# Local scores of tiles 6 and 11 moved one step behind the values, and the last output block stored in halves

## The chip, the cores and the metric

The kernel runs on one core of a Trainium2 chip. The metric is the device time of one execution in microseconds. It is measured several times per kernel, and one more execution is profiled. Engines are named as in the profile: PE (TensorE; PEld are its weight loads), DVE (VectorE), ACT (ScalarE), POOL (GpSimd) and SP (SyncE, which issues the DMAs).

## The reference

Attention with two kinds of heads, followed by a feed-forward layer on all tokens:

```python
batch, n_heads, seq, head_dim = (8, 8, 576, 64)
scores = scale * np.matmul(q, k.transpose(0, 1, 3, 2))
rel = pos[:, None] - pos[None, :]
mask_local = (rel >= 0) & (rel < stride)
mask_strided = (rel >= 0) & (pos[None, :] % stride == pos[:, None] % stride)
masks = np.stack([mask_local if h < H // 2 else mask_strided for h in range(H)], axis=0)
attn = softmax(np.where(masks, scores, -1e9))
x = (attn @ v) as 4608 tokens x 512 channels
h = x @ w_in
out = (0.5 * h * (1 + erf(h / sqrt(2)))) @ w_out
```

The stride is 32, w_in is 512 x 2048 and w_out 2048 x 512, all in float32.

## The kernel before

The 4608 tokens are cut into 12 tiles of 384. A tile has three local jobs of 128 tokens each (heads 0 to 3), strided rows (heads 4 to 7) and 16 steps of feed-forward, one for each 128 of the 2048 hidden channels. Steps are numbered through: n = 16 t + f. Values are kept as a high part rounded for PE and a low remainder (xh and xl, gh and gl), so each product is three matmuls.

- **Feed-forward step n.** `ffn_h` (L619 to L621) makes 12 matmuls of 128x384 into a PSUM bank H. `ffn_g` applies Gelu on ACT (L628), rounds to gh on ACT (L630) and subtracts to gl on DVE (L632). `ffn_o` of step n-2 (L658 to L660) makes 9 matmuls of 128x512 into three banks O. `store` copies O to SBUF on ACT (L665) and sends it from SP (L667) once a tile is full.
- **Strided heads.** They run on DVE alone: dot products row by row (L494, two instructions each), and accumulations of weighted values (L536), cut into small pieces that `run_strided` hands out step by step; a transpose (L544), then xh on ACT (L236) and xl on DVE (L238).
- **Local heads.** A `band_job` has seven parts. Part 0 is the score matmuls (L297; the page counts 96 passes for the three jobs of a tile). Parts 1 to 3 are the masked minimum on DVE (L311), the exponential on ACT (L315), and on DVE the quotients and a transpose, with 8 small DMAs per job from SP that set up the tile `band` (L326). Part 4 is the value matmuls (L337; 48 passes per tile). Parts 5 and 6 copy the result to xh on ACT (L236) and subtract xl on DVE (L238).

A tile's scores stand in two PSUM banks S0 and S1 of 512 columns: 128 columns for each of the three jobs. The last 128 columns of the *next* tile's two banks take the values of the third job of *this* tile; the other two jobs' values go to a bank X. Before, `score_banks` took a tile's two banks in the step in which its scores were made.

The order on ACT and PE is the order of the code in `step(n)`: first `visit(n)` (value matmuls of one tile, then score matmuls of the next), then `ffn_h(n)` and its Gelu, then the softmax parts due in this step, strided pieces, and `ffn_o(n-2)`. Which step visits which tile is set by three tables:

```python
    FIRST, VISIT = 2, 13
    value_at = {ready[t - 1] + VISIT: t for t in range(2, NTILE)}
    score_at = {ready[1] + FIRST: 2, **{n: t + 1 for n, t in value_at.items()}}
    soft_at = {}
    for n, t in score_at.items():
        for i in range(JPT if t < NTILE else 0):
            for p in (1, 2, 3):
                soft_at.setdefault(n + p + i * (2 if t == 2 else 4), []).append((t * JPT + i, p))
```

With `ready[t] = 16 t`, step 77 has the values of tile 5 and the scores of tile 6, step 157 the values of tile 10 and the scores of tile 11, and step 173 the values of tile 11 alone. DVE's, SP's and POOL's order is worked out by the framework's scheduler from the same code; the framework also sets the semaphore waits between engines, for any two accesses of one PSUM tile.

Of the kernel before, what the change touches and what calls it, by code (L numbers as in the profile page):

```python
# [24 lines left out]
P = 128  # L25
STRIDE = 32
TT = 384
# [55 lines left out]
def attn_ffn_kernel(ctx: ExitStack, tc: tile.TileContext, qk, vl, qka, va, qs, ks, vs, w, out):  # L83
    nc = tc.nc
# [4 lines left out]
    NT, DM = out.shape  # L89
# [4 lines left out]
    NTILE = NT // TT  # L94
# [32 lines left out]
    def slot(name, shape, dtype=F32):  # L127

        return wpool.tile(shape, dtype, name=name, tag="w")
# [149 lines left out]
    def score_banks(t):  # L279
        return [ps_a.tile([P, DM], F32, name=f"S{j}_{t}", tag=f"S{j}") for j in range(2)]  # L280
# [165 lines left out]
    for vi in range(NA, NV):  # L446
        n = VISITS[vi][2]
# [162 lines left out]
    hps, gs, ops_ = {}, {}, {}  # L610
    ready = [t * NF for t in range(NTILE)]
# [23 lines left out]
    def runs(t, a):  # L635

        res = []
        for c in range(0, P, 32):
            _, b, r = ROWS[TR * t + (a * P + c) // 32]
            r = b * S + 32 * r  # L640
            if res and res[-1][2] + res[-1][1] - res[-1][0] == r:
                res[-1][1] = c + 32
            else:
                res.append([c, c + 32, r])
        return res
# [16 lines left out]
    def store(t):  # L662
        for a in range(TT // P):
            ob = opool.tile([P, DM], F32, name=f"ob_{t}_{a}", tag="ob", bufs=3)
            nc.scalar.copy(ob, ops_[t][a])  # L665
            for c0, c1, r0 in runs(t, a):
                nc.sync.dma_start(out[r0:r0 + c1 - c0, :], ob[c0:c1, :])  # L667


    strided = []  # L670
# [2 lines left out]
    for u in range(U0, NU + 1):  # L673
        for v, what, names in ((u, strided_qk, "qk"), (u - 1, strided_av, "v")):
            if U0 <= v < NU:
                vi, _, r0, nr, t, _ = PLACE[v]
# [39 lines left out]
    t = slot("pbig", [P, 4 * DM])  # L716
# [27 lines left out]
    for i in range(JPT):  # L744
        t = opool.tile([P, DM], F32, name=f"first_{i}", tag="ob", bufs=3)
# [3 lines left out]
    def ffn(n):  # L749
        ffn_h(n)  # L750
        yield
        yield from ffn_g(n)
        yield
        ffn_o(n)
        if n % NF == NF - 1:
            yield
            store(n // NF)
# [39 lines left out]

    FIRST, VISIT = 2, 13  # L800
    value_at = {ready[t - 1] + VISIT: t for t in range(2, NTILE)}
    score_at = {ready[1] + FIRST: 2, **{n: t + 1 for n, t in value_at.items()}}
    soft_at = {}
    for n, t in score_at.items():
        for i in range(JPT if t < NTILE else 0):
# [5 lines left out]
    banks = {}  # L811
# [6 lines left out]
    def part(x, *which):  # L818

        for p in which:  # L820
            if p == 0:
                local[x] = [band_job(x, bts[x % NBT], banks), 0]
            assert local[x][1] == p
            local[x][1] += 1
            next(local[x][0], None)
            if p == 0:
                load_jq(x + 3)

    def visit(n):

        t = value_at.get(n, 0)
        if score_at.get(n, 0):
            banks[score_at[n]] = score_banks(score_at[n])
        for i in range(JPT if t else 0):
            part(t * JPT + i, 4)
        for i in range(JPT if score_at.get(n, NTILE) < NTILE else 0):
            part(score_at[n] * JPT + i, 0)
# [12 lines left out]
    def step(n):  # L850


        c = n // NF
        visit(n)
        if NB <= n < NS:
            ffn_h(n)
            for _ in ffn_g(n):
                pass
        old = len(splits)
        while old and n >= xfree[splits[0][0]]:  # L860
            for _ in splits.pop(0)[1]():
                pass
            old -= 1
        softmaxes(n)
        flush_exps(NU)
        if c + 1 < NTILE:
            a, e = ready[c] + (1 if c == 0 else 0), ready[c + 1]
            part_of = min(1.0, max(0.0, (n - a + 1) / (e - a - 3)))
            need = last[c] + (last[c + 1] - last[c] + sum(taken[a:e - 3])) * part_of - sum(taken[a:min(n + 1, e - 3)])
            share = (n + 1 - NB) / (ready[-1] - 2 - NB)  # L870
            run_strided(max(need, (tot + sum(taken)) * share - sum(taken[:n + 1])))
        if n == NS + 1:
            ffn_o(n - 3, n - 2)
        elif n >= NB + 2 and n < NS:
            ffn_o(n - 2)
        if n >= NB + 2 and (n - 2) % NF == NF - 1:
            store((n - 2) // NF)
# [71 lines left out]
```

## Time and profile before

| what | value |
|---|---|
| runs | 875.07, 878.97, 878.74 us; median 878.74 |
| profiled execution | 877.5 us, its span 875.7 us |
| mean granted TensorE clock | 0.990 |
| busy: PE, DVE, ACT | 856.4 us (98%), 706.2 us (81%), 482.7 us (55%) |
| chain that ended last | PE 90%, DVE 3%, DMA 3%, ACT 2% |
| H matmuls L619, L620, L621 | 768 each, 261.6, 259.4 and 260.6 us |
| O matmuls L658, L659, L660 | 576 each, 224.4, 227.7 and 228.3 us |
| score matmuls L297 | 1056, 13.8 us |

How to read it: the span goes from the first to the last instruction on any engine; the execution's own time has a little more around it. The chain is followed back from the last instruction to what released it at each step. "Issue" is time in which an engine waited for nothing that the profile shows. Busy shares are averages over the whole span; what a place is worth is read from the timeline there.

### The profile page before, as it was taken

How to read it: one execution, taken by the hardware profiler on the slowest of the kernel's cores; microseconds unless marked ns; L12 is line 12 of the kernel's file. 1: busy time of each engine (PE TensorE's matmuls, PEld its weight loads, DVE VectorE, ACT ScalarE, POOL GpSimd, SP SyncE). 2: the span in 40 equal slices, each digit the busy share in tenths (PEclk: the TensorE clock that was granted, in tenths of full speed). 3: DMA queues.
4: the chain of work that ended last, by engine and by line, in shares of the span. 5: the costliest groups of instructions: out<-in, count | busy, mean ns of one | idle time of the engine just before them, and what ended most of it. 6: DMA issues, size and time to landing. Idle time of an engine off the chain costs nothing.

```text
span 875.7 us, 19634 instructions
## 1 busy us (share of the span) xinstructions
PE 856.4 (98%) x6082; PEld 771.0 (88%) x6082; DVE 706.2 (81%) x4901; ACT 482.7 (55%) x1001; POOL 17.5 (2%) x89
## 2 busy tenths in 40 slices
PE   5999999999999999999999999999999989999998
PEld 4888898999999999999999899989989979989997
DVE  6998999998989997889999979899799993751111
ACT  7888585566465375357355445556547435443222
POOL 5000100000000000000000000000000000000000
PEclk9799999999999999999999999999999999999999
DMA  9695301320310320310311121131032002000001
GB/s 352 223 380 200 115 24 37 108 76 8 128 47 9 101 97 10 104 44 8 97 50 58 55 76 47 34 122 48 9 101 80 12 30 59 18 6 12 26 1 37
DMA packets 34552, 66.67 MB, mean 76 GB/s; under 512 B 6800, under 2 KB 16528, under 8 KB 34448
## 3 DMA queue, kind: packets, MB, share of 16 engines
q1 hardware_dynamic: 34448, 65.43, 22.1%
q8 instruction: 48, 0.79, 0.4%
q14 instruction: 56, 0.46, 0.2%
HBM read 51.64 MB, written 9.44 MB: 70 GB/s over the span
## 4 chain that ended last, share of the span: by engine, by line
PE 90%; DVE 3%; DMA 3%; ACT 2%; SPq 1%; issue 1%; DVEq 0%; ACTq 0%
PE H L619 15%; PE O L659 14%; PE O L660 14%; PE H L621 14%; PE H L620 14%; PE O L658 14%; PE X_L L337 1%; PE S L297 1%; DMA ws<-in_w_dram 1%; DMA qka<-in_qka_dram 1%; DMA sk<-in_ks_dram 1%; DVE ws L161 1%; SPq L326 1%; PE S L337 1%; DVE w L169 1%
## 5 line engine op out<-in xcount | busy, mean ns | idle before, releaser
L628 ACT ACTIVATE H<-H 128x384 f32<-128x384 f32 x192 | 91.3, 476 | 363.0 <-PE H L621 304.3
L619 PE MATMUL H<-xh,w 128*128 128x384 f32 x768 | 261.6, 341 | 1.5 <-DVE gl L632 1.4
L621 PE MATMUL H<-xh,w 128*128 128x384 f32 x768 | 260.6, 339 | 0.0
L620 PE MATMUL H<-xl,w 128*128 128x384 f32 x768 | 259.4, 338 | 0.4 <-DVE xl L238 0.4
L536 DVE SCALAR_TENSOR_TENSOR acc<-sv,sc,acc 128x64 f32<-128x64 f32 x1158 | 249.5, 275 | 0.7
L660 PE MATMUL O<-w,gl 128*128 128x512 f32 x576 | 228.3, 396 | 0.0
L659 PE MATMUL O<-w,gh 128*128 128x512 f32 x576 | 227.7, 395 | 0.0
L658 PE MATMUL O<-w,gh 128*128 128x512 f32 x576 | 224.4, 390 | 0.0
L494 DVE CUSTOM_DVE_ANT_0 junk<-sq,sk 128x64 f32<-128x64 f32 x1290 | 203.8, 217 | 3.5 <-DMA sk<-in_ks_dram 2.4
L632 DVE TENSOR_TENSOR gl<-H,gh 128x384 fp32r<-128x384 f32 x192 | 105.7, 551 | 106.0 <-ACT gh L630 105.1
L619 PEld LDWEIGHTS H<-xh,w 128*128 128x128 f32 x768 | 145.4, 189 | 11.1 <-DVE gl L632 1.7
L620 PEld LDWEIGHTS H<-xl,w 128*128 128x128 f32 x768 | 145.3, 189 | 8.5 <-DVE xl L238 0.8
L621 PEld LDWEIGHTS H<-xh,w 128*128 128x128 f32 x768 | 145.0, 189 | 0.1
L660 PEld LDWEIGHTS O<-w,gl 128*128 128x128 f32 x576 | 108.1, 188 | 23.7 <-DVE gl L632 0.6
L659 PEld LDWEIGHTS O<-w,gh 128*128 128x128 f32 x576 | 108.1, 188 | 18.2
L658 PEld LDWEIGHTS O<-w,gh 128*128 128x128 f32 x576 | 108.5, 188 | 17.3
L494 DVE DVE_READ_ACCUMULATOR2_ANT sc<- 128x1 f32 x1290 | 103.6, 80 | 0.0
L630 ACT CAST gh<-H 128x384 fp32r<-128x384 f32 x192 | 92.2, 480 | 6.1
L628 ACT ACT_TABLE_LOAD x60 | 77.0, 1283 | 1.0
L504 ACT ACT_TABLE_LOAD x35 | 44.9, 1283 | 0.6
L315 ACT ACTIVATE PT_L<-P_L,nm_L 128x64 f32<-128x64 f32 x132 | 44.2, 337 | 0.3
L315 ACT ACT_TABLE_LOAD x24 | 30.8, 1283 | 0.5
(114 smaller groups left out, 488.7 us busy)
## 6 DMA issues: line engine op xcount, KB each, us to landing
ws<-in_w_dram SPq DMA_DIRECT2D x16, 1023.8 KB, 10.1
qk<-in_qk_dram SPq DMA_DIRECT2D x36, 320.0 KB, 5.0
out_dram<-ob SPq DMA_DIRECT2D x34, 256.0 KB, 2.4
vl<-in_vl_dram SPq DMA_DIRECT2D x36, 192.0 KB, 4.3
sk<-in_ks_dram SPq DMA_DIRECT2D x8, 576.0 KB, 5.5
sv<-in_vs_dram SPq DMA_DIRECT2D x8, 576.0 KB, 3.9
band<-PT_L SPq DMA_DIRECT2D x240, 16.0 KB, 1.8
sq<-in_qs_dram SPq DMA_DIRECT2D x4, 576.0 KB, 4.4
```

The source lines that it names most:

```text
L315: nc.scalar.activation(pv[:, :, h, :], p1[:, h * 2 * QB:(h + 1) * 2 * QB].rearrange("p (c t) -> p c t", c=2), AF.Exp, bias=nm[:, h:h + 1], ...
L494: nc.vector.tensor_tensor_reduce(junk, sq[vi, "q"][:, r0 + r, :], sq[vi, "k"][:, c, :], 1.0, 0.0, ALU.mult, ALU.add, ss[u][:, r, c:c + 1])
L536: nc.vector.scalar_tensor_tensor(acc[:, r, :], sq[vi, "v"][:, c, :], wgt, acc[:, r, :], ALU.mult, ALU.add)
L619: nc.tensor.matmul(hp, w1[f][:, 0, c, :], xh[:, c, :], start=(c == 0), stop=False)
L620: nc.tensor.matmul(hp, w1[f][:, 0, c, :], xl[:, c, :], start=False, stop=False)
L621: nc.tensor.matmul(hp, w1[f][:, 1, c, :], xh[:, c, :], start=False, stop=(c == NC - 1))
L628: nc.scalar.activation(hp, hp, AF.Gelu)
L630: nc.scalar.copy(gh, hp)
L632: nc.vector.tensor_tensor(gl, hp, gh.bitcast(F32), ALU.subtract)
L658: nc.tensor.matmul(o, gh[:, sl], w2[f][:, 0, :], start=(f == 0), stop=False)
L659: nc.tensor.matmul(o, gh[:, sl], w2[f][:, 1, :], start=False, stop=False)
L660: nc.tensor.matmul(o, gl[:, sl], w2[f][:, 0, :], start=False, stop=(f == NF - 1))
```

## The change

`LATE` names the tiles 6 and 11. Their scores (part 0) are made in the step behind the one that has the values of the tile before: step 78 instead of 77, and step 158 instead of 157. Softmax parts follow, since `soft_at` counts from `score_at`. The two S banks are still taken in the values' step, since the values' third job writes into them. In `store`, the last 128 tokens of the last tile are copied in two halves of 256 columns, the first on ACT and the second on DVE, each with its own DMA.

```diff
-            nc.scalar.copy(ob, ops_[t][a])
-            for c0, c1, r0 in runs(t, a):
-                nc.sync.dma_start(out[r0:r0 + c1 - c0, :], ob[c0:c1, :])
+            halves = 2 if t == NTILE - 1 and a == TT // P - 1 else 1
+            for i in range(halves):
+                cs = slice(i * DM // halves, (i + 1) * DM // halves)
+                if i:
+                    nc.vector.tensor_copy(ob[:, cs], ops_[t][a][:, cs])
+                else:
+                    nc.scalar.copy(ob[:, cs], ops_[t][a][:, cs])
+                for c0, c1, r0 in runs(t, a):
+                    nc.sync.dma_start(out[r0:r0 + c1 - c0, cs], ob[c0:c1, cs])
...
-    FIRST, VISIT = 2, 13
+    FIRST, VISIT, LATE = 2, 13, (6, 11)
     value_at = {ready[t - 1] + VISIT: t for t in range(2, NTILE)}
-    score_at = {ready[1] + FIRST: 2, **{n: t + 1 for n, t in value_at.items()}}
+    score_at = {ready[1] + FIRST: 2, **{n + (t + 1 in LATE): t + 1 for n, t in value_at.items()}}
...
         t = value_at.get(n, 0)
-        if score_at.get(n, 0):
-            banks[score_at[n]] = score_banks(score_at[n])
+        new = t + 1 if t else score_at.get(n, 0)
+        if new and new not in banks:
+            banks[new] = score_banks(new)
```

PE, tile 6: the last value matmuls and the first score matmuls, with the semaphores that each waits for. S_6 are tile 6's two banks, O_2 is the last of the three output banks. Before:

```order
L337 MATMUL S_6_5581<-band,vl_4551 64x64
L337 MATMUL S_6_5582<-band,vl_4551 64x64 [waits PE_49]
L337 MATMUL S_6_5582<-band,vl_4551 64x64 x3
L297 MATMUL S_6_5581<-qk_4569 32x64
L297 MATMUL S_6_5582<-qk_4569 32x64
```

Now, behind the value matmuls, 12 matmuls of H and 9 of O:

```order
L658 MATMUL O_2_4975<-w_1222,gh_5504 128x512
L659 MATMUL O_2_4975<-w_1222,gh_5504 128x512
L660 MATMUL O_2_4975<-w_1222,gl_5505 128x512
L297 MATMUL S_6_5581<-qk_4569 32x64 [waits DVE_49]
L297 MATMUL S_6_5582<-qk_4569 32x64 [waits DVE_49]
```

The scores stood directly behind the values and now stand a step later, and the first one into each bank waits for DVE: the counts waited for are those of the two `xl<-S_6` below. At tile 11 the same two rows stand in the same way.

DVE, tile 6: gl of step 77, then xl of the three jobs' values (X_L: two jobs, S_6: the third job in two halves). Before (between the gl of the step before and this one stand 22 of L536, L544 and 23 pairs of L494):

```order
L632 TENSOR_TENSOR gl_5682<-H_5668,gh_5681 128x384
L494 ISA junk_3_5_6127,sc_6038<-sq_5459,sk_5461 128x64
...
L238 TENSOR_TENSOR xl_4817<-X_L_5583,xh_4816 128x2x128 x2
L238 TENSOR_TENSOR xl_4817<-S_6_5581,xh_4816 128x128
L311 ISA P_L_5728,nm_L_5730<-S_6_5581,bmaskNone 128x64
...
L238 TENSOR_TENSOR xl_4817<-S_6_5582,xh_4816 128x128
```

Now (between the two gl stand 22 of L536, L544 and 6 pairs of L494):

```order
L632 TENSOR_TENSOR gl_5628<-H_5614,gh_5627 128x384
L494 ISA junk_2_1_6050,sc_5994<-sq_5459,sk_5461 128x64
...
L238 TENSOR_TENSOR xl_4817<-X_L_5583,xh_4816 128x2x128 x2
L238 TENSOR_TENSOR xl_4817<-S_6_5581,xh_4816 128x128
L238 TENSOR_TENSOR xl_4817<-S_6_5582,xh_4816 128x128
```

Each fence shows the first of four L494 pairs that stand between gl and xl. Up to the gl of step 76 DVE's order is the same in both kernels; then gl and xl stand 17 pairs earlier, and the two xl of S_6 follow each other.

DVE, tile 11: the same place at step 157. Before:

```order
L503 TENSOR_TENSOR sc_11469<-sc_11469,m_11610 128x36
L536 SCALAR_TENSOR_TENSOR acc_11328<-sv_10030,sc_10676,acc_11328 128x64 x25
L632 TENSOR_TENSOR gl_10974<-H_10960,gh_10973 128x384
L536 SCALAR_TENSOR_TENSOR acc_11328<-sv_10030,sc_10676,acc_11328 128x64 x2
L238 TENSOR_TENSOR xl_10070<-X_L_10881,xh_10069 128x2x128 x2
L238 TENSOR_TENSOR xl_10070<-S_11_10879,xh_10069 128x128
```

Now:

```order
L503 TENSOR_TENSOR sc_11469<-sc_11469,m_11570 128x36
L536 SCALAR_TENSOR_TENSOR acc_11319<-sv_10030,sc_10676,acc_11319 128x64 x5
L632 TENSOR_TENSOR gl_10926<-H_10912,gh_10925 128x384
L536 SCALAR_TENSOR_TENSOR acc_11319<-sv_10030,sc_10676,acc_11319 128x64 x2
L238 TENSOR_TENSOR xl_10070<-X_L_10881,xh_10069 128x2x128 x2
L238 TENSOR_TENSOR xl_10070<-S_11_10879,xh_10069 128x128
L238 TENSOR_TENSOR xl_10070<-S_11_10880,xh_10069 128x128
```

Of the 25 accumulations ahead of gl, 20 stand behind it now, and up to L503 the order is the same.

On ACT there are 126 table loads where there were 120, since softmax parts and strided exponentials fall into other steps. At the end, DVE's copy of the second half waits for ACT's count after the first half, and SP issues the two DMAs one behind the other.

## Rows read from the trace of the kernel before

**Rows 1.** The page, part 1: busy us (share) xinstructions of each engine

```profile
PE 856.4 (98%) x6082; PEld 771.0 (88%) x6082; DVE 706.2 (81%) x4901; ACT 482.7 (55%) x1001; POOL 17.5 (2%) x89
```

**Rows 2.** Timeline of PE, 707 to 724 us: start us, us, engine, line, operation

```profile
707.53 0.33 PE L619 MATMUL H<-xh,w 128*128 128x384 f32 x1
...
717.44 0.30 PE L297 MATMUL S<-qk 64*32 64x64 f32 x4 [2.94 <-issue]
...
723.52 0.33 PE L619 MATMUL H<-xh,w 128*128 128x384 f32 x1
```

**Rows 3.** Stretches: length, busy of PE, PEld, DVE, ACT, POOL; PEclk, DMA, GB/s

```profile
718.60:722.05 3.45, 3.45 (x12) 3.25 (x11) 3.06 (x16) 0.84 (x2) 0.00 (x0) 0.51 0.02 5
82.50:87.30 4.80, 3.42 (x18) 3.20 (x19) 4.77 (x20) 4.61 (x9) 0.00 (x0) 1.00 0.09 21
```

**Rows 4.** Timeline of PE, tile 6's visit: first H matmul of steps 76, 77, 78

```profile
358.36 0.33 PE L619 MATMUL H<-xh,w 128*128 128x384 f32 x1
...
365.29 0.44 PE L619 MATMUL H<-xh,w 128*128 128x384 f32 x1
...
369.58 0.33 PE L619 MATMUL H<-xh,w 128*128 128x384 f32 x1
```

**Rows 5.** Timeline of PE, values-only visit: first H matmul of steps 171 to 174

```profile
777.95 0.33 PE L619 MATMUL H<-xh,w 128*128 128x384 f32 x1
...
782.14 0.33 PE L619 MATMUL H<-xh,w 128*128 128x384 f32 x1
...
787.97 0.44 PE L619 MATMUL H<-xh,w 128*128 128x384 f32 x1
...
792.26 0.33 PE L619 MATMUL H<-xh,w 128*128 128x384 f32 x1
```

**Rows 6.** The chain of waits at a visit: start us, us, engine and line

```profile
432.55 1.08 PE X_L L337 x32
433.63 0.47 PE S L337 x16
```

**Rows 7.** DMA queues, whole span and then 714.8 to 716 us: packets, MB, share

```profile
q8 instruction: 48, 0.79, 0.4%
...
q8 instruction: 1, 0.02, 5.4%
```

**Rows 8.** Timeline of DVE, 368 to 373 us (tile 6)

```profile
368.48 0.22 DVE L494 CUSTOM_DVE_ANT_0 junk<-sq,sk 128x64 f32<-128x64 f32 x1
...
370.96 0.55 DVE L632 TENSOR_TENSOR gl<-H,gh 128x384 fp32r<-128x384 f32 x1
...
372.01 0.75 DVE L238 TENSOR_TENSOR xl<-X_L,xh 128x256 fp32r<-128x256 f32 x2
372.68 0.28 DVE L238 TENSOR_TENSOR xl<-S,xh 128x128 fp32r<-128x128 f32 x1
```

**Rows 9.** Timeline of DVE, 716 to 724 us (tile 11)

```profile
716.68 4.98 DVE L536 SCALAR_TENSOR_TENSOR acc<-sv,sc,acc 128x64 f32<-128x64 f32 x25
722.19 0.56 DVE L632 TENSOR_TENSOR gl<-H,gh 128x384 fp32r<-128x384 f32 x1 [0.54 <-ACT gh L630]
...
723.06 0.75 DVE L238 TENSOR_TENSOR xl<-X_L,xh 128x256 fp32r<-128x256 f32 x2
```

**Rows 10.** Timeline of ACT, 365 to 370 us (tile 6)

```profile
369.11 0.47 ACT L236 CAST xh<-S 128x128 fp32r<-128x128 f32 x2
```

**Rows 11.** Timeline of DVE, 790 to 794 us (values-only visit)

```profile
792.81 0.48 DVE L238 TENSOR_TENSOR xl<-S,xh 128x128 fp32r<-128x128 f32 x2
```

**Rows 12.** ACT's table loads (count, busy us, mean ns); last copy on ACT; output DMAs

```profile
L628 ACT ACT_TABLE_LOAD x60 | 77.0, 1283 | 1.0
...
871.90 0.59 ACT L665 COPY ob<-O 128x512 f32<-128x512 f32 x1 [0.77 <-PE O L660]
...
DMA to landing us min/median/max: 2.0/2.4/3.3
```

## The prediction

> **What bounds the kernel now.** I read the page's engine table first: PE is busy 98% of the span [rows 1], so only what makes PE idle, slows it or adds work to it moves the end. Next I read PE's timeline at the edited places. PE's stream is a row of equal steps of 4.19 us (from one step's first H matmul to the next, 777.95 to 782.14 [rows 5]). In one step of each tile stands a "visit": 48 value passes of this tile (L337), then 96 score passes of the next (L297). At tile 6's visit two steps take 369.58 - 358.36 = 11.22 us [rows 4], less two plain steps 8.38: the visit costs 2.84 us. At tile 11's visit the same two steps take 723.52 - 707.53 = 15.99 us [rows 2], so 7.61, which is 4.77 more. Of this 2.94 us are a gap with four score passes left, put down to "issue" [rows 2]; the remaining 1.83 us come right behind it, where the granted clock is 0.51 for some 3.4 us, the 1.2 GHz level [rows 3]. This is the one place in the middle of the kernel where the profiled execution loses time; tile 6's visit loses none.
>
> Then I read the DMA view for that gap. Queue q8 brings PE's instructions: 48 packets, 0.79 MB in the span [rows 7], 16 KB each. PE has 6,082 matmuls [rows 1], each with a weight load, so a packet holds 12,164 / 48, about 250 of these. A visit issues 2 x (48 + 96) = 288 in under 3 us: more than one packet, where a plain step issues 42 in 4.19 us. One packet falls into 714.8 to 716 us, inside the gap [rows 7]. I take the gap as PE waiting for its next packet. The Trainium skill (Runtime: NRT & Kernel Launch, "Instruction fetch mechanics") says that instructions are refilled in 16 KiB blocks, fetched while the current one runs and mostly hidden. Packet size and trace agree; "mostly hidden" doesn't hold here, since the gap is 2.94 us. By that rule the gap would have another cause and would stay, and the time would be that of case 3 below.
>
> **The change, part by part.**
>
> *The gap at tile 11, removed: -4.77 us.* With the scores a step later the block has 96 instructions, then a plain step of 42, then 192; each piece is less than a packet, and over 4 us lie between. Bounds: 0 (it stays) and 4.77. I take 4.77, the row itself.
>
> *Two blocks where there was one: +0.4 us.* Values alone cost 792.26 - 782.14 - 8.38 = 1.74 us at the last visit [rows 5]; their matmuls take 1.08 + 0.47 = 1.55 [rows 6], so 0.19 goes into entering and leaving a block of small matmuls. Beside values the scores cost 2.84 - 1.74 = 1.10; alone 1.29. That is 0.19 per tile, twice, 0.4. Ends: 0 and 0.6.
>
> *A new wait, before the scores.* The order of the changed kernel shows it: the first score matmul of tile 6 into each S bank now waits for DVE, at tile 11 too. It waits for L238's xl, which subtracts the third job's values out of columns 384 to 511 of the same bank. Before, scores stood directly behind the values and waited for nothing. PE takes its work in order, so H and O of the next step stand behind the wait. Its price:
>
> Tile 6. Behind a values-only block the next H starts 787.97 - 782.14 = 5.83 us after the last [rows 5]: 358.36 + 5.83 = 364.19. PE is ready for the scores one H and O later, 369.58 - 365.29 = 4.29 us [rows 4]: at 368.48. ACT's last xh ends 4.29 us after its H's start too (369.11 + 0.47 against 365.29) [rows 10, 4]: 368.48, just in time. DVE is what is late. Up to gl of the step before, its order is unchanged; behind it stand 22 accumulations, a transpose and six L494 pairs, then gl. The seventh pair starts at 368.48 in the trace [rows 8], so gl starts there. From gl through four pairs to xl takes 372.01 - 370.96 = 1.05 us, the two X parts 372.68 - 372.01 = 0.67 [rows 8], the two S parts 0.48 [rows 11]: the second ends at 370.68. PE waits 2.2 us.
>
> Tile 11. H at 707.53 + 5.83 = 713.36, PE ready at 717.65. DVE's order now has gl behind 5 accumulations where 25 stood. They begin at 716.68, 0.20 us each [rows 9]: gl at 717.68; gl and two accumulations 723.06 - 722.19 = 0.87 [rows 9], then 0.67 + 0.48 as above: 719.70. PE waits 2.05 us.
>
> Together +4.25. Lower end: with DVE idle beforehand, xl at the last visit ended 792.81 + 0.48 - 787.97 = 5.32 us behind its H [rows 11, 5], against 4.29: 1.03 each, 2.1 together. Upper end 2.94 each, 5.9, the largest gap in this stretch. I take 4.25, from DVE's own rows at these places.
>
> That the wait is by bank and not by column is what the Trainium skill asks for (PSUM — Partial Sum Buffer, "PSUM bank collisions raise a hardware error"): two engines must not touch one bank and quadrant at once, even in other columns. With a wait by column the sum would be the lower end of case 2; no row of the trace before shows the case.
>
> *The clock behind the new waits: +1.83 us.* A gap of 2.94 us was followed by the 1.2 GHz level, which cost 1.83 [rows 2, 3]; one of 1.38 us from 82.5 us on was followed by full clock [rows 3]. Gaps of 2.05 and 2.2 lie between the two. Ends: 0 and 3.66. I take one fall of two, 1.83.
>
> *The rest of the moved work: 0.* Softmax, 24 band DMAs and three qk loads on SP follow one step later for these two tiles, four steps (16.8 us) before the values need them instead of five, and no wait of PE depends on less. ACT gets 126 table loads instead of 120, 6 x 1.28 = 7.7 us [rows 12], spread over dozens of steps and hidden since O takes gh and gl two steps behind H; without that cover, 7.7.
>
> *The last store: 0.* ACT copies half of 512 columns, DVE the other half. The order has the DVE copy wait for ACT's, so they don't run side by side. 0.59 us [rows 12] becomes, at half the width, 0.3 to 0.4 on ACT and then about 0.4 on DVE (gl of 384 columns takes 0.55 [rows 8]): some 0.2 us later than before, with both DMAs behind one queue. Half as many bytes may land sooner; store landings range from 2.0 to 3.3 us [rows 12], the median 2.4. Ends -0.4 and +0.5; I take 0.
>
> **Sum**, against the profiled execution's own 877.5 us (span 875.7 and 1.8 around it): 877.5 - 4.77 + 0.4 + 4.25 + 1.83 + 0 = **879.2 us**. The median of the runs shown is 878.74, 1.2 above that execution, and they lie between 875.07 and 878.97; a spread of 3.9 is about one such gap, so runs probably differ in it. A gap removed and two waits put in its place: no change that can be told. What a measurement of this kernel can tell from no change is about 0.5%, 4.4 us: below 874.3 or above 883.1.
>
> **Forecast and rivals.**
>
> 1. *Forecast.* Both waits at about 2 us; with no fall of the clock 877.4, one 879.2, two 881.0. Chance 0.64. Its own range is 876.5 to 882.
>
> 2. *Faster: the waits are short.* If DVE reaches xl as early as at the last visit, they are 1.03 each, too short to cost clock: 877.5 - 4.77 + 0.4 + 2.06 = 875.2; with no wait at all 873.1. For it: DVE is busy only 81% of the span [rows 1]. Against: in both places its rows leave no gap up to where gl now stands [rows 8, 9]. It decides if xl ends less than 1.5 us behind PE's ready time. Chance 0.16, which also holds runs of the kernel before with a dearer gap than the profiled one.
>
> 3. *Slower: the gap at tile 11 isn't cured.* If it is no late packet, or the packet now comes late for the 192 scores, 2.94 and the clock stay and the waits come on top: 879.2 + 4.77 = 884.0. For it: the packet's request isn't in the trace, only its transfer. The Trainium skill's rule on fetches, above, would have it so. Against: PE now has 4.29 us and the wait itself between the blocks. It decides if the packet is asked for only when the scores begin. Chance 0.13.
>
> 4. *The change adds only.* If the unprofiled runs mostly lack the gap, as the one at 875.07 may, the new waits are a loss against them: 875.07 + 0.4 + 4.25 + 1.83 = 881.6, or 883.4 with a second fall. Chance 0.07.
>
> **Range and chances.** The low end 875.0 takes in the short waits, the high end 883.0 both falls of the clock and the median's 1.2 us on top, with some room; what lies outside is no wait at all and case 3. Faster 0.15 (the lower part of case 2, and dear gaps before), slower 0.15 (case 3, and the end of case 4), the same 0.70.
>
> **What would show it.** Right: no "issue" gap at tile 11's scores; in their place, at tiles 6 and 11, PE idle by about 2 us before the first L297, released by DVE xl L238; a stretch of clock near 0.5 behind one of them; two steps around each split at 3.0 us plus the wait over plain ones. Wrong: waits under 1 us, or no row of PE waiting on xl; "issue" again inside a block; PE waiting on gl. At the end, DVE's copy starting before ACT's has ended.

## The result, and the profile after

The changed kernel takes 879.37 us (median of 22 runs, 877.36 to 882.27), the kernel before in the same comparison 877.54 us (22 runs, 874.61 to 880.53). The ratio is 1.0025, 95% interval 1.0013 to 1.0036: 2.2 us slower, within the 0.5% that counts as no change. The predicted 879.2 us was 0.2 us off.

The profiled execution of the changed kernel took 881.07 us, its span 879.3. The page's engine table, against [rows 1]:

```profile
PE 857.8 (98%) x6082; PEld 770.5 (88%) x6082; DVE 706.6 (80%) x4902; ACT 490.4 (56%) x1007; POOL 17.6 (2%) x89
```

PE has the same 6,082 passes. ACT has 1,007 instructions where it had 1,001, the six table loads, and DVE one copy more. What PE waited for (engine, line, releaser: us in total, times, longest):

```profile
PE S L297 <- DMA qk<-in_qk_dram: 5.7, 1, 5.7
PE S L297 <- DVE xl L238: 3.5, 2, 1.9
```

The second line is the new wait, twice. The "issue" gap of [rows 2] has no line here any more. The first line belongs to the start of the kernel, about which more below. PE's timeline at tile 6 (beside [rows 4]) and at tile 11 (beside [rows 2]):

```profile
364.73 1.15 PE L337 MATMUL X_L<-band,vl 96*64 96x64 f32 x32
365.71 0.64 PE L337 MATMUL S<-band,vl 96*64 96x64 f32 x16
366.28 0.44 PE L619 MATMUL H<-xh,w 128*128 128x384 f32 x1
...
372.62 1.56 PE L297 MATMUL S<-qk 64*32 64x64 f32 x96 [1.89 <-DVE xl L238]
...
717.80 1.15 PE L337 MATMUL X_L<-band,vl 96*64 96x64 f32 x32
718.78 0.72 PE L337 MATMUL S<-band,vl 96*64 96x64 f32 x16
719.43 0.44 PE L619 MATMUL H<-xh,w 128*128 128x384 f32 x1
...
725.51 1.35 PE L297 MATMUL S<-qk 64*32 64x64 f32 x96 [1.64 <-DVE xl L238]
```

All 96 score passes now run in one piece, and PE stands idle ahead of them for 1.89 and 1.64 us, until DVE has xl. DVE's timeline at the two places:

```profile
370.57 0.55 DVE L632 TENSOR_TENSOR gl<-H,gh 128x384 fp32r<-128x384 f32 x1
...
371.62 0.75 DVE L238 TENSOR_TENSOR xl<-X_L,xh 128x256 fp32r<-128x256 f32 x2
372.28 0.48 DVE L238 TENSOR_TENSOR xl<-S,xh 128x128 fp32r<-128x128 f32 x2
...
723.65 0.54 DVE L632 TENSOR_TENSOR gl<-H,gh 128x384 fp32r<-128x384 f32 x1
...
724.51 0.74 DVE L238 TENSOR_TENSOR xl<-X_L,xh 128x256 fp32r<-128x256 f32 x2
725.18 0.47 DVE L238 TENSOR_TENSOR xl<-S,xh 128x128 fp32r<-128x128 f32 x2
```

At tile 6 both xl of S end at 372.28 + 0.48 = 372.76, the scores having begun at 372.62 on the first bank. gl, X parts and S parts follow each other as the prediction laid them out. The clock in the two gaps and behind them (length; busy time and count of PE, PEld, DVE, ACT, POOL; PEclk, DMA share, GB/s):

```profile
370.73:372.62 1.89, 0.00 (x2) 0.00 (x1) 1.89 (x13) 0.00 (x0) 0.00 (x0) 1.00 0.81 287
372.62:376.10 3.48, 3.48 (x102) 3.25 (x103) 3.48 (x48) 0.00 (x0) 0.00 (x0) 0.62 0.43 108
723.87:725.51 1.64, 0.00 (x1) 0.01 (x1) 1.64 (x7) 0.00 (x0) 0.00 (x0) 1.00 0.00 0
725.51:729.00 3.49, 3.49 (x109) 3.34 (x110) 3.49 (x27) 0.00 (x0) 0.00 (x0) 1.00 0.02 5
```

Behind tile 6's wait the granted clock falls (0.62 is a mean over a stretch that is partly at the 1.2 GHz level), behind tile 11's it doesn't. The last copies, ACT's and DVE's (beside [rows 12]):

```profile
875.24 0.37 ACT L672 COPY ob<-O 128x256 f32<-128x256 f32 x1 [0.77 <-PE O L660]
875.65 0.42 DVE L670 COPY ob<-O 128x256 f32<-128x256 f32 x1 [4.99 <-ACT ob L672]
```

They run one after the other. From PE's last matmul (its end at 875.20) to the end of the span it is 4.09 us now, 3.87 before.

Two places carry the comparison, so I read their cost from every profiled execution in the same way: from the first weight load of H in the step before the visit to that three steps later, less three plain steps (12.57 us). For tile 11 in the changed kernel: 730.83 - 713.29 - 12.57 = 4.97.

| profiled execution | tile 6, us | tile 11, us |
|---|---|---|
| kernel before | 2.84 | 7.61 |
| changed kernel | 6.64 | 4.97 |
| changed kernel, profiled once more | 5.17 | 4.98 |
| changed kernel, 16 more lead-in rounds | 5.16 | 4.97 |
| only tile 11 split | 2.82 | 4.97 |
| only tile 6 split | 5.16 | 4.52 (gap of 1.40) |
| only the halves | 2.82 | 3.66 (gap of 0.48) |
| before, 16 more lead-in rounds | 2.84 | 2.84 (no gap) |
| before, 24 more lead-in rounds | 2.82 | 2.82 (no gap) |
| scores two steps late at both | 3.16 | 3.21 |

A visit without gap or wait costs 2.83. Split, it costs 5.16 at tile 6 and 4.97 at tile 11, and 1.48 more where the clock falls behind it. Unsplit, tile 11 costs 3.66, 4.52 or 7.61, by the length of its gap. Between step 16 and the last matmul the profiled executions of before and of the change differ by at most 0.1 us over all other steps, so these two columns, the start and the tail hold the whole difference.

### The profile page after: what moved, and what is told of

Read it like the earlier page. It is cut to its first block, busy times and chain, and to the rows that moved or that the text cites. A ratio compares the mean times of both kernels' runs of the same rounds, so it can differ in the third digit from the quotient of the medians.

```text
span 879.3 us, 19643 instructions
## 1 busy us (share of the span) xinstructions
PE 857.8 (98%) x6082; PEld 770.5 (88%) x6082; DVE 706.6 (80%) x4902; ACT 490.4 (56%) x1007; POOL 17.6 (2%) x89
## 4 chain that ended last, share of the span: by engine, by line
PE 83%; DVE 8%; DMA 5%; ACT 2%; issue 1%; SPq 0%; DVEq 0%; ACTq 0%
PE H L619 14%; PE H L621 13%; PE H L620 13%; PE O L659 13%; PE O L660 13%; PE O L658 13%; DVE acc L536 3%; DMA ws<-in_w_dram 3%; DVE junk L494 1%; PE S L297 1%; DMA qk<-in_qk_dram 1%; PE X_L L337 1%; DMA qka<-in_qka_dram 1%; DVE w L169 1%; DVE gl L632 1%; DVE ws L161 1%
## 5 line engine op out<-in xcount | busy, mean ns | idle before, releaser
L536 DVE SCALAR_TENSOR_TENSOR acc<-sv,sc,acc 128x64 f32<-128x64 f32 x1158 | 250.2, 276 | 0.8
L494 DVE CUSTOM_DVE_ANT_0 junk<-sq,sk 128x64 f32<-128x64 f32 x1290 | 204.7, 217 | 2.9 <-issue 1.4
L494 DVE DVE_READ_ACCUMULATOR2_ANT sc<- 128x1 f32 x1290 | 104.0, 81 | 0.0
```

The source lines that it names most:

```text
L494: nc.vector.tensor_tensor_reduce(junk, sq[vi, "q"][:, r0 + r, :], sq[vi, "k"][:, c, :], 1.0, 0.0, ALU.mult, ALU.add, ss[u][:, r, c:c + 1])
L536: nc.vector.scalar_tensor_tensor(acc[:, r, :], sq[vi, "v"][:, c, :], wgt, acc[:, r, :], ALU.mult, ALU.add)
```

## The experiments

The theory: the change takes away a gap that comes from PE's instruction packets, and pays it back with two waits for DVE's xl. Rivals: the split itself costs; the gap has another cause; the halves matter.

**Parts alone.** Tile 11 alone, tile 6 alone and the halves alone. The first:

```diff
-    FIRST, VISIT = 2, 13
+    FIRST, VISIT, LATE = 2, 13, (11,)
-    score_at = {ready[1] + FIRST: 2, **{n: t + 1 for n, t in value_at.items()}}
+    score_at = {ready[1] + FIRST: 2, **{n + 1 * (t + 1 in LATE): t + 1 for n, t in value_at.items()}}
```

The second has `(6,)` in the same place; both take `score_banks` as the change does. The third has the change's new `store` and none of its tables.

> The change for tile 11 alone, without the split store. Theory: gap gone, -4.8; second block +0.2; a wait of PE for DVE xl of 1.6 to 2.1 us; clock falls behind it in some runs only, +0 to +1.8. Sum -2.8 without a fall, -0.7 with one. Rival (the split itself costs, wherever it stands, and the gap was worth nothing in unprofiled runs): +2 us or more.

> The change for tile 6 alone, without the split store. Theory: nothing to cure there, so only cost: second block +0.2, wait for DVE xl about 2 us, clock falls in about half of the runs or more, 0 to +1.8; the gap at tile 11 stays. Sum +2.1 to +4.0. Rival (tile 6 has the same late packet in unprofiled runs, so its split also cures something): -2 to +1 us.

> The last store in halves alone. Theory: ACT's copy about 0.35 us, then DVE's about 0.4 behind it, not beside it; the second DMA is issued some 0.2 us later than the single one was and carries half; time the same within 0.4 us. Rival (halves land sooner and the end moves with them): about -0.5 us, the last landing earlier against PE's last matmul.

Measured, beside 34 runs of the kernel before (876.62 us, 873.64 to 882.43):

| kernel | median (range), us | ratio, 95% interval |
|---|---|---|
| tile 11 alone | 877.01 (874.86 to 879.70) | 1.0010 (0.9994 to 1.0026) |
| tile 6 alone | 879.53 (876.74 to 885.76) | 1.0043 (1.0022 to 1.0064) |
| halves alone | 876.55 (873.53 to 879.25) | 0.9999 (0.9978 to 1.0019) |

Tile 11 alone trades its gap for its wait and comes out even (0.9 us more, -0.5 to 2.3 by the interval); 0.7 to 2.8 us less was expected, with the gap taken at its full 4.8. Tile 6 alone has no gap to trade and loses 3.8 us (1.9 to 5.6 by the interval); its profile shows 2.3 at the visit, and the rest is not accounted for. The halves are worth nothing either way. PE's timeline with tile 11 alone, the score block at tile 11:

```profile
721.17 1.35 PE L297 MATMUL S<-qk 64*32 64x64 f32 x96 [1.65 <-DVE xl L238]
```

With tile 6 alone, the score blocks at tiles 6 and 11:

```profile
373.24 1.35 PE L297 MATMUL S<-qk 64*32 64x64 f32 x96 [1.89 <-DVE xl L238]
...
718.52 1.14 PE L297 MATMUL S<-qk 64*32 64x64 f32 x92
721.06 0.30 PE L297 MATMUL S<-qk 64*32 64x64 f32 x4 [1.40 <-issue]
```

With the halves alone, tile 11:

```profile
714.13 1.14 PE L297 MATMUL S<-qk 64*32 64x64 f32 x92
715.75 0.30 PE L297 MATMUL S<-qk 64*32 64x64 f32 x4 [0.48 <-issue]
```

The waits come back from profile to profile, to 0.01 us here and to 0.06 in all five profiles that have them. The gap stands in the same place each time, with 4 of 96 passes left as in [rows 2], but its length is 2.94, 1.40 or 0.48 us. The DMA view shows what differs. With the halves alone, 713 to 714.2 us (queue: packets, MB, share):

```profile
q8 instruction: 1, 0.02, 4.6%
q1 hardware_dynamic: 1, 0.00, 0.5%
```

Here the instruction packet goes ahead of a load of values (vl, three DMAs of 192 KB on q1, which SP begins to issue 0.7 us after the visit's first matmul in all three executions): one packet of q1 moved beside it. In the kernel before, whose visit began 0.7 us earlier (711.82), 70 packets of q1 and none of q8 moved in that stretch; q8's began at 714.91 [rows 7]:

```profile
q1 hardware_dynamic: 70, 0.14, 43.9%
```

In each of the three executions the last four passes start 1.3 to 1.5 us after the packet's transfer has ended, by the packet's own record in the trace: at 715.75 behind 714.33 (halves alone), 721.06 behind 719.75 (tile 6 alone), 717.44 behind 715.94 (before). So the gap ends with the packet. That the load makes the packet late is not shown: these three would fit it, the two gaps made below don't.

**Moving the packets.** The kernel before, with nothing changed but the number of matmuls that PE runs on zeros at the very start. A round issues two matmuls and two weight loads, so 16 rounds are 64 instructions more ahead of everything. The profile has 12,315 instructions of PE, semaphores included, and 48 packets bring them, some 256 to a packet. Tile 11's block has 298 instructions with its semaphores, and the gap stands ahead of the last eight (four passes with their weight loads). If that is where a packet ends, at 290, the one before it ended at 34, in the same block. With 64 more instructions ahead, the end at tile 11 moves to 226, and the nearest to a block's start is tile 7's, at 18.

```diff
-    for i in range(49):
+    for i in range(65):
```

> The kernel before with 16 more of the tiny matmuls that keep PE busy while the first inputs load; nothing else. They add 64 instructions to PE's stream ahead of everything, so that packets end 64 instructions earlier in every block. Theory (the gap at tile 11 is PE waiting for an instruction packet, because the second of two packet ends falls just inside the block of 288): no gap at tile 11 and none elsewhere, since no block then has its first packet end some 34 to 38 instructions in; time about 4.8 us under the kernel before (2.9 if the clock doesn't fall behind the gap in the run compared). Rival (the gap comes from the place: the vl loads that start in this block, or the matmuls themselves): gap of about 2.9 us at tile 11 as before, time the same within 0.5 us.

Measured: 874.41 us (873.53 to 875.37, 12 runs), ratio 0.9977, interval 0.9966 to 0.9989. PE's timeline at tile 11:

```profile
713.40 1.15 PE L337 MATMUL X_L<-band,vl 96*64 96x64 f32 x32
714.38 0.64 PE L337 MATMUL S<-band,vl 96*64 96x64 f32 x16
714.95 1.17 PE L297 MATMUL S<-qk 64*32 64x64 f32 x96
```

No gap. The ratio gives the gap's worth in timed runs, as the shift as a whole shows it: 2.0 us on average (1.0 to 3.0 by the interval), less than the 4.8 or 2.9 expected. The runs lie within 1.8 us, those of the halves, as many and with the gap, within 5.7. This kernel is the fastest of all that ran, and beats both the one before and the change.

To rule out that more lead-in is good in itself, the next one shifts by half as much again. Counted as above, packets then end 34 instructions into tile 3's block and 38 into tile 8's.

```diff
-    for i in range(49):
+    for i in range(73):
```

> The kernel before with 24 more lead-in matmuls in place of the 16 of the run that lost the gap at tile 11. Theory (the gap belongs to the place where a packet of TensorE's instructions ends inside the split visit's block of 48 short matmuls): the packet ends move on by half as much again and now lie early in the block at tile 3's visit (about 153 us) and in that at tile 8's visit (about 502 us): 'issue' gaps ahead of L297 of 0.5 to 2.9 us at one or both of these, none at tile 11; 876 to 880 us, slower than the run with 16 more by 1.5 to 5 us. Rival (the gap belongs to tile 11, by its loads or its place late in the span): a gap of 0.5 to 2.9 us again at tile 11 and none at tiles 3 and 8; 876 to 878 us. Second rival (more lead-in is itself what made the run with 16 faster): no gap anywhere, 874 us or less.

Measured: 887.00 us (883.29 to 889.47, 6 runs), ratio 1.0099 (1.0071 to 1.0127). PE's timeline at tiles 3, 8 and 11:

```profile
161.67 1.14 PE L297 MATMUL S<-qk 64*32 64x64 f32 x92
164.23 0.30 PE L297 MATMUL S<-qk 64*32 64x64 f32 x4 [1.42 <-issue]
...
512.53 1.15 PE L297 MATMUL S<-qk 64*32 64x64 f32 x94
515.66 0.27 PE L297 MATMUL S<-qk 64*32 64x64 f32 x2 [1.98 <-issue]
...
725.23 1.17 PE L297 MATMUL S<-qk 64*32 64x64 f32 x96
```

The gaps appear at the two tiles named beforehand and are gone from tile 11; with the packet's end four instructions later in the block (38), two passes fewer are left. The place belongs to the packet and not to the tile. The time, though, is 7 us above the top of what was expected. The profile says where: PE's waits have two more "issue" entries at the start of the kernel, where I hadn't counted.

```profile
PE S L297 <- issue: 5.9, 3, 2.5
PE A L430 <- issue: 3.5, 1, 3.5
```

Of the 5.9 us, 2.5 fall at 27 us and the 3.5 at 19 us. Against the kernel with 16 rounds more, step 45 begins 7.5 us later (234.28 against 226.83), of which 1.8 are tile 3's gap; tile 8 adds 2.3. Moving packets can hurt elsewhere as much as it helps.

**Where the price of the split lies.** Scores two steps late instead of one, at both tiles, the last block stored whole:

```diff
-    score_at = {ready[1] + FIRST: 2, **{n: t + 1 for n, t in value_at.items()}}
+    score_at = {ready[1] + FIRST: 2, **{n + 2 * (t + 1 in LATE): t + 1 for n, t in value_at.items()}}
```

> The change's split at tiles 6 and 11, but the scores two steps behind the values in place of one, and the last block stored whole. Theory (the change's added cost is the wait for DVE's copy of the values, xl, which holds the banks one step on and no longer two steps on): no idle time of TensorE over 0.3 us ahead of the first L297 at either tile, no 'issue' gap at tile 11, no fall of the clock in either place; 874.5 to 875.5 us, that is 4 us under the change and about 2 under the kernel before. Rival (the split itself costs, by more block changes, more loads of ACT's table or late scores that hold up ACT's exponentials): 877 to 880 us with no wait for xl in the trace.

Measured: 876.91 us (875.88 to 878.71, 12 runs), ratio 0.9991 (0.9975 to 1.0007). PE's timeline at tile 6, then 436 us, 657 us and tile 11:

```profile
374.67 1.17 PE L297 MATMUL S<-qk 64*32 64x64 f32 x96
...
436.69 0.57 PE L337 MATMUL S<-band,vl 96*64 96x64 f32 x12 [0.48 <-DMA band<-PT_L]
...
657.55 0.44 PE L619 MATMUL H<-xh,w 128*128 128x384 f32 x1 [1.18 <-DVE gl L632]
...
726.79 1.17 PE L297 MATMUL S<-qk 64*32 64x64 f32 x96
```

Neither score block waits, there is no gap, and over four steps the split costs 0.2 us a tile. So the wait for xl is what costs in the change, and the split by itself little, as the theory has it. But the kernel was expected at 874.5 to 875.5 and stands 1.4 above. In its profile 0.7 us goes at 436 us, where tile 6's band is not ready for its values (a wait of 0.48 for the last of its DMAs), 0.8 in two steps where O waits for ACT's copies of outputs, and 1.6 at 657 us behind gl. The first follows from the second step of delay; that the third does, one profile can't show.

**The change again, and with the packets moved.** The change unaltered, and the change with the 16 lead-in rounds:

```diff
-    for i in range(49):
+    for i in range(65):
```

> The change once more, unaltered, so that it stands on the same chip and beside the same runs of the kernel before as the other three: 878 to 880 us by every theory; waits of 1.6 to 2.2 us for xl at tiles 6 and 11, no 'issue' gap at tile 11.

> The change with the 16 more lead-in matmuls that by themselves took the gap at tile 11 from the kernel before: here nothing is left at tile 11 for them to take. Theory (the change gains the gap and pays it back in waits): the same time as the change, 878 to 880 us, about 4 to 5 us above the kernel before with 16 more lead-ins, which is the whole price of the split at two tiles: two waits of 1.6 to 2.0 us, 0.4 us of block changes, and one fall of the clock or none. Rival (the change still loses time to packets at some other visit): 876 to 877 us, and an 'issue' gap in the change's own trace that is not in this one's.

Measured, beside 29 runs of before (877.21 us, 874.55 to 881.31): the change 879.03 (877.39 to 881.23), ratio 1.0019 (1.0004 to 1.0034); with the shift 879.26 (877.20 to 880.99), ratio 1.0023 (1.0007 to 1.0039). The shift that is worth 2 us to the kernel before is worth nothing to the change: the gap it takes away is already gone. Set beside the gapless kernel before, the whole split costs 1.0023 / 0.9977 = 1.0046, 4.0 us; the profiles' two columns give 5.16 + 4.97 - 2 x 2.83 = 4.47. What PE waited for, in the change profiled once more:

```profile
PE S L297 <- DVE xl L238: 3.6, 2, 1.9
```

And the stretches behind its two waits, of 1.90 and 1.66 us:

```profile
370.51:373.99 3.48, 3.48 (x109) 3.33 (x110) 3.48 (x48) 0.00 (x0) 0.00 (x0) 1.00 0.46 153
...
721.76:725.24 3.48, 3.48 (x109) 3.32 (x109) 3.48 (x27) 0.00 (x0) 0.00 (x0) 1.00 0.02 5
```

The clock stayed at full speed behind both.

## Why the prediction was right, point by point

The forecast's mechanism is what the profiles show, and its time came out to 0.2 us. Two of its terms were mis-sized all the same, the gap by 2.8 us too much gain and the clock by 1.4 us too much cost, and they cancel in part. The mechanism was right; that the time is met to 0.2 us is luck.

- **The gap at tile 11, -4.77.** Its cause is confirmed: a late instruction packet. The two shifts of the lead-in show it, one by removing the gap and one by making two others in the tiles that the count named. Case 3, the gap not cured, falls. The Trainium skill (Runtime: NRT & Kernel Launch, "Instruction fetch mechanics") has the fetches mostly hidden; here they aren't, by 0.48 to 2.94 us in five gaps. The size was taken from one execution, whose gap was the longest of the three profiled and the only one with a clock fall behind it. Over timed runs the gap is worth 2.0 us, and 12 of the 34 runs of the kernel before beside it lie no higher than the highest of the gapless kernel (875.37), as case 4 would have it for a part of the runs. The prediction suspected this ("runs probably differ in it") but summed with the full 4.77, against an execution that without its gap would have stood at 872.7, below every run of the gapless kernel (873.53 to 875.37).
- **Two blocks instead of one, +0.4.** With the scores two steps late, 0.2 us a tile: as said.
- **The new waits, +4.25.** Named right in place, releaser and order. PE's idle rows are 1.89 and 1.64, predicted 2.2 and 2.05. Their cost to the end is a little more than the row, since a block of scores takes 1.35 us behind a wait and 1.17 without: 5.16 - 2.83 - 0.2 = 2.13 at tile 6, 4.97 - 2.83 - 0.2 = 1.94 at tile 11, together 4.07. The reckoning from DVE's own rows held to 0.2 us; DVE's head start of case 2 (1.03 each) isn't there, nor is its lower end, no wait at all.
- **The clock, +1.83, one fall of two.** Seen just so in the first profile, behind tile 6, where it cost 6.64 - 5.16 = 1.48 us. The 1.83 of the prediction had more in it: the gaps of 0.48 and 1.40 us, with no fall behind them, cost 0.3 us beyond their length too (4.52 - 2.83 - 1.40). But in the two other profiles of the split at both tiles, and in the two of one tile, it didn't fall: one fall behind eight waits. As an average the term is nearer 1.48 x 2 / 8 = 0.4 us for the change.
- **The rest of the moved work, 0.** Right for the time: PE waits 0.4 us on ACT's gh once in the first profile, at 61.5 us and so before either split, and nothing else moved.
- **The last store, 0.** The halves alone give 0.9999 (0.9978 to 1.0019); the tail is 0.2 us longer, by the copies running one behind the other. Right.

So against a gapless kernel the change pays 0.4 + 4.07 + 0.4 for its split and 0.2 at the tail, about 5; measured, by the two ratios with the shift, 4.0 (the intervals of both together allow about 1.7 us either way). Against the kernel before it gets 2.0 back, and +2.2 us stands as the result. In the profiled pair the span grew by 3.6 us, and it is not all the change: +3.80 at tile 6, -2.64 at tile 11, +0.2 in the tail, and +2.0 before the first step (its first H weight load at 28.49 against 26.53), where PE waits for the first qk load. That start varies between 26.5 and 28.5 us in nine of the ten profiles, those of the kernel before and of the same change included, so it says nothing on the change.

## What to carry to other kernels

A gap put down to "issue" inside a dense block of short instructions can be an instruction packet that comes late, and moving the stream by a few dozen instructions at its start is a cheaper test, and here a better cure, than reordering the work; count where the packets then end in the other blocks, the start of the kernel included. Before work is moved behind an operation that shares its buffer, find the engine that releases the buffer and add up its queue from its own rows: here that gave the cost of the new wait to 0.1 us a tile. A one-off gap in one profiled execution has a length, not a price: take its worth from the spread of the runs or from a run without it.

## What the runs showed that I had not expected

- The gap's length goes with the end of the packet's transfer. From the visit's first value matmul to that end it was 1.83, 2.80 and 4.13 us at tile 11 (halves alone, tile 6 alone, before) and 2.68 and 3.23 in the two gaps of the kernel with 24 rounds; the gaps were 0.48, 1.40, 2.94, 1.42 and 1.98, each 1.2 to 1.4 us shorter. PE went on 1.3 to 1.5 us after the transfer had ended in these two as well (164.23 behind 162.72, 515.66 behind 514.15). The order of packet and load doesn't decide: the packet of the 1.98 us gap began ahead of its vl load (512.55 against 512.60), that of the shorter 1.42 us gap with packets of loads already moving. What sets the time at which a packet comes stays open.
- Without the gap and without new waits the 12 runs of the kernel before with 16 rounds lie within 1.8 us; with the gap 12 runs of the halves lie within 5.7, and with the waits 12 of the change within 3.8. That one late packet makes a good part of a kernel's scatter fits this and isn't shown: the 12 runs with the scores two steps late have neither and lie within 2.8, those of tile 11 alone have no gap and lie within 4.8.
- In the kernel before a packet also ends 30 instructions into tile 6's block, four earlier than at tile 11, and there is no gap there [rows 4]. The packet was early there: its transfer ran from 361.09 to 362.37 us, ahead of the visit's first matmul at 362.64. So it was at tile 7 with 16 rounds (an end at 18): 431.85 to 433.08, and 433.69. In all five gaps it began 0.9 to 3.1 us behind that matmul. Why four instructions decide it was not tried.
- The clock fell behind one wait of 1.89 us and stayed up behind three others of 1.89 to 1.90 us at the same place of the program. What decides it stays open.
